# A fourth seven-product step of w_out in each late tile, the first product copied by ScalarE, and the casts placed one half step later

## The chip, the cores and the metric

The kernel runs on one core of one Trainium2 chip. The metric is the device time of one execution in microseconds (us), lower is better. Engines are named as the profile names them: PE is TensorE (matrix products, into PSUM), PEld its weight loads, DVE is VectorE, ACT is ScalarE, POOL is GpSimd, SP issues transfers.

## What is computed

The input has 8 batches of 3008 tokens of 256 numbers. A spectral mixing step (Fourier transform along the tokens, a complex 256x256 product with a bias, soft shrinkage, inverse transform) makes 24064 tokens, on which a dense two-layer network runs:

```python
def _moe_ref(x, w_in, w_out):          # x: 24064 x 256, w_in: 256 x 2048, w_out: 2048 x 256
    h = x @ w_in
    r = np.maximum(h, 0.0)
    g = r * r
    return (g @ w_out).astype(np.float32)

attn_out = _attn_ref(**attn_kwargs)    # rfft, complex product and bias, shrinkage, irfft
out = _moe_ref(x=attn_out.reshape(B * S, D), **moe_kwargs)
```

## The kernel before, in words

**Tiles and steps.** The tokens are cut into 48 tiles (six per batch) of 500 or 504 tokens, in two halves of `h` = 250 or 252. The 2048 hidden columns go in 8 steps of 256, so a tile has steps 0 to 7 and the program 384. Numbers are fp32; every product is made of three matrix products of reduced-precision parts ("high" and "low" parts of both sides, hence tiles in pairs such as `mg0`, `mg1`).

**One step.** The first product of a step is w_in times the tile. A 2x2 block product is made with seven block products instead of eight, by sums of blocks: `Step.first` issues four of them (12 matmuls into the PSUM banks psh0 and psh1), `Step.second` the other three (9 matmuls, psh2 and psh3). VectorE puts them together: it copies the first product to SBUF (`p1`, tile `mp`), adds it to the second (`u2`, tile `mu`), adds that to a pair (`v`, tile `mv`), and makes four rectified sums into the tile `mc`, by `rectified` (shown as CUSTOM_DVE_ANT_0 in the trace, as ISA in an instruction order). One of the four is made in `first`; in `second` there are two, first `c[:, 1:3]` from `psh2` and `v`, then `c[:, 0]` from `psh3` and `p1`. So `p1` is still read at the very end of `second`. The tile `mp` has one buffer (the table `MAIN` says `"mp": 1`). The end of `second` then gives out the casts: ScalarE squares `mc` in place and casts it to the high part `mg0`, GpSimd subtracts to get the low part `mg1`.

**w_out, plain and seven.** `Step.out` multiplies with w_out: 12 matmuls of 500 columns into the two accumulators `pso0` and `pso1`. It runs two half steps behind: in the main loop (one pass `m` per half step) TensorE gets `first` of step n, half of `out` of n - 2, the other half, `second` of n, and so on. In the tiles 38 to 46 (`FREE`), where the work of the mixing step is over, the steps in `SEVEN` (1, 3, 5) take seven block products here too (`out_seven`): 21 matmuls of 250 columns. They need four sums of the blocks of `mc`, which `forms` makes: three VectorE operations into `ftt`, two ScalarE casts to the high parts `fth`, two GpSimd subtractions to the low parts `ftl`. Parts of the seven products pile up over the tile in two banks (`psf`), and `tile_sums` (four VectorE operations into `mo`) unfolds them once, in the tile after; the last `out` of a tile then adds its accumulators (two VectorE operations on `mo`) and stores.

**Weights of the sums.** `out_sums(n)` makes, for each step in `SEVEN`, the sums of the w_out blocks: six GpSimd operations and one ScalarE cast, in the tiles before 38, placed by a time in a list of jobs.

**Next tile.** In the late tiles the input of the following tile is split into parts by `Tokens.free`, given out around the casts of steps 0, 2, 4 and 6, as pieces: sums `ts` at step 0, and at the later steps a ScalarE cast to `yt0` with a GpSimd subtraction to `yt1`.

**What sets the order.** `then` chains each operation behind the one given out before it on its engine, so within an engine the order is that of the program text; nothing on an engine overtakes.

Of the kernel before, what the change touches and what calls it, by code (L numbers as in the profile page):

```python
# [11 lines left out]
F32R = mybir.dt.float32r  # L12
# [20 lines left out]
NF = FF // 128  # L33
# [25 lines left out]
TURN0, TURNS, PACE = 92, J, 6  # L59
FREE = range(ENDS * len(HALF) + 2, B * len(HALF) - 1)  # L60
SPARE = 6
SEVEN = (1, 3, 5)


@with_exitstack
def fnet_moe(ctx: ExitStack, tc, x, w_r, w_i, b2, w_in, w_out, bm, cm, dx, am2, a32, c32, d32, out):
# [34 lines left out]
    def T(name, shape, dt, tag=None):  # L101
        tag = tag or name
        return pools.get(tag, phase["pool"]).tile(shape, dt, name=name, tag=tag, bufs=phase["bufs"].get(tag, 2))
# [72 lines left out]
    def halves(hi, lo, v, eng):  # L176
        copy(act, hi, v)
        sub(eng, lo, v, hi)
# [416 lines left out]
    class Tokens:  # L595
# [3 lines left out]
        def free(self, n, behind):  # L599
            y, h = raw[self.t], self.h  # L600
            if n == 0 and not behind:
                self.s = T("ts", [128, 1024], F32)[:, :4 * h].rearrange("p (j h) -> p j h", j=4)
                yts[self.t] = [
                    T(f"yt{j}", [128, 7 * HM], F32R)[:, :7 * h].rearrange("p (j h) -> p j h", j=7) for j in range(2)
                ]
            s = self.s
            if n == 0:
                if not behind:
                    then(pool, sub, pool, s[:, 0], y[:, 0, h:2 * h], y[:, 0, :h])
                    then(pool, sub, pool, s[:, 1], y[:, 1, h:2 * h], y[:, 0, h:2 * h])  # L610
                else:
                    then(pool, pool.tensor_add, out=s[:, 2], in0=y[:, 0, :h], in1=s[:, 1])
                    then(pool, sub, pool, s[:, 3], y[:, 1, :h], s[:, 2])
                return
            pieces = {
                (2, False): (B11, 1, y[:, 0, :h].unsqueeze(1)),
                (2, True): (B21, 2, y[:, 1, :2 * h].rearrange("p (j h) -> p j h", j=2)),
                (4, False): (T1, 2, s[:, 0:2]),
                (6, False): (T2, 2, s[:, 2:4]),
            }  # L620
            if (n, behind) in pieces:
                b, j, v = pieces[n, behind]
                js = slice(b, b + j)
                yh, yl = yts[self.t]
                then(act, copy, act, yh[:, js], v)
                then(pool, sub, pool, yl[:, js], v, yh[:, js])
# [53 lines left out]
    ws = []  # L680

    def out_sums(n):
        if not ws:
            ws.extend(T(name, [128, len(SEVEN), 4, 128], F32R) for name in ("wsh", "wsl"))
        i = SEVEN.index(n)
        st = T("st", [128, 1024], F32, tag="tt")
        w = st[:, :512].rearrange("p (f e d) -> p f e d", f=2, e=2)
        s = st[:, 512:].rearrange("p (j d) -> p j d", j=4)
        pool.tensor_add(out=st[:, :512].rearrange("p (f d) -> p f d", f=2), in0=wout[0][:, 2 * n:2 * n + 2], in1=wout[1][:, 2 * n:2 * n + 2])
        a11, a21, a12, a22 = w[:, 0, 0], w[:, 0, 1], w[:, 1, 0], w[:, 1, 1]  # L690
        pool.tensor_add(out=s[:, 0], in0=a21, in1=a22)
        sub(pool, s[:, 1], s[:, 0], a11)
        sub(pool, s[:, 2], a11, a21)
        sub(pool, s[:, 3], a12, s[:, 1])
        halves(ws[0][:, i], ws[1][:, i], s, pool)

    def tile_sums(t):
        h = tiles[t][2]
# [10 lines left out]
    class Step:  # L709
# [12 lines left out]
        def first(self):  # L722
            h = self.h
            self.ps = pa, pb, pc, pd = [bank([128, 2, 256], f"psh{j}")[:, :, :h] for j in range(4)]
            self.p1 = p1 = T("mp", [128, HM], F32)[:, :h]
            u2 = T("mu", [128, HM], F32)[:, :h]
            self.v = v = T("mv", [128, 2 * HM], F32)[:, :2 * h].rearrange("p (j h) -> p j h", j=2)
            self.c = c = T("mc", [128, 4 * HM], F32)[:, :4 * h].rearrange("p (j h) -> p j h", j=4)
            self.product(pa[:, 0], A11, B11)
            if self.t + self.n == 0:  # L730
                m4, m6, m3 = (pd[:, 0], A12, B21), (pc[:, 0], S4, B22), (pb[:, 0], S1, T1)
                m5, m2, m7 = (pb[:, 1], S3, T3), (pa[:, 1], S2, T2), (pc[:, 1], A22, T4)
                for m, terms in (
                    (m4, (0, 1, 2)), (m6, (0, 1, 2)), (m3, (0, 1)), (None, 4), (m2, (0, 1)), (m3, (2,)),
                    (m5, (0, 1, 2)), (m7, (0, 1)), (m2, (2,)), (m7, (2,)), (None, 3),
                ):
                    if m:
                        self.product(*m, terms)
                    else:
                        awake(terms, then)  # L740
            else:
                self.product(pa[:, 1], S2, T2)
                self.product(pb[:, 0], S1, T1)
                self.product(pb[:, 1], S3, T3)
            then(dve, copy, dve, p1, pa[:, 0])
            then(dve, dve.tensor_add, out=u2, in0=pa[:, 1], in1=p1)
            then(dve, dve.tensor_add, out=v, in0=pb, in1=u2.unsqueeze(1).broadcast_to([128, 2, h]))
            self.rectified(c[:, 3], pb[:, 0], v[:, 1])
# [4 lines left out]
        def second(self):  # L753
            h, c = self.h, self.c
            pc, pd = self.ps[2:]
            if self.end:
                return self.finish(pc, pd)
            if self.t + self.n:
                self.product(pc[:, 0], S4, B22)
                self.product(pc[:, 1], A22, T4)  # L760
                self.product(pd[:, 0], A12, B21)
            self.rectified(c[:, 1:3], pc, self.v)
            self.rectified(c[:, 0], pd[:, 0], self.p1)
            self.cut = last_of[dve]
            self.g = g = [
                T(f"mg{j}", [128, 4 * HM], F32R)[:, :4 * h].rearrange("p (j h) -> p j h", j=4) for j in range(2)
            ]
            then(act, act.activation, c, c, AF.Square)
            then(act, copy, act, g[0], c)
            self.bent = last_of[act]  # L770
            for j in (slice(0, 1), slice(2, 4)) if self.seven else (slice(0, 2), slice(2, 4)):
                then(pool, sub, pool, g[1][:, j], c[:, j], g[0][:, j])
            self.low = last_of[pool]
# [14 lines left out]
        def out_seven(self, j):  # L788
            t, h, n = self.t, self.h, self.n
            i, begins = SEVEN.index(n), n == self.sevens[0]  # L790
            if begins and j == 0:
                part[t] = [bank([128, 512])[:, :2 * h].rearrange("p (j h) -> p j h", j=2) for _ in range(2)]
            low, high = [a[:, :2 * h].rearrange("p (j h) -> p j h", j=2) for a in acc[t]]
            p16, p57 = part[t]
            f = 2 * n
            plain = [[w[:, f + k, d * 128:(d + 1) * 128] for w in wout] for d, k in ((0, 0), (0, 1), (1, 1))]
            sums = [[w[:, i, k] for w in ws] for k in range(4)]
            g, tf = self.g, (self.th, self.tl)
            if j == 0:
                todo = ((p16[:, 0], plain[0], g, 0), (low[:, 0], plain[1], g, 2), (low[:, 1], sums[3], g, 3))  # L800
            else:
                todo = (
                    (p57[:, 0], sums[0], tf, 0), (p57[:, 1], sums[2], tf, 1),
                    (p16[:, 1], sums[1], tf, 2), (high[:, 0], plain[2], tf, 3),
                )
            for q, (x, y) in enumerate(((0, 0), (1, 0), (0, 1))):
                for at, (ps, a, b, k) in enumerate(todo):
                    then(
                        pe, pe.matmul, ps, a[x], b[y][:, k],
                        start=begins and q == at == 0, stop=i == len(SEVEN) - 1 and q == 2 and j == 1 and at in (1, 2),  # L810
                    )
# [206 lines left out]
    for r in range(-1, len(units) + 3):  # L1018
# [5 lines left out]
        k = r - 2  # L1024
# [103 lines left out]
    for m in range(2 * len(steps) + 4):  # L1128
# [1 line left out]
        if k and 0 <= n - 2 < len(steps):  # L1130
            steps[n - 2].out(1)
        if n < len(steps):
            t, i = divmod(n, NF // 2)
            ahead = k and t in FREE and i in (0, 2, 4, 6)
            if ahead:
                if i == 0:
                    tokens = Tokens(t + 1)
                tokens.free(i, False)
            (steps[n].second if k else steps[n].first)()
            if ahead:  # L1140
                tokens.free(i, True)
            if not k and n and steps[n - 1].seven:
                steps[n - 1].forms()
            if not k and n % (NF // 2) == 0 and steps[n].t - 1 in FREE:
                tile_sums(steps[n].t - 1)
        if not k and 0 <= n - 2 < len(steps):
            steps[n - 2].out(0)
        if m in LATER:
# [103 lines left out]
```

## Time and profile before

| | |
|---|---|
| three runs, us | 2565.12, 2564.72, 2565.14; median 2565.12 |
| the profiled execution, us | 2564.88, of which its span is 2563.1 |
| TensorE busy | 2553.7 us (100%), its granted clock full throughout (9 in every slice) |
| VectorE, ScalarE, GpSimd busy | 74%, 55%, 68% |
| chain that ended last | 97% TensorE, 1% VectorE, 1% transfers |

"Busy" of an engine is the time in which one of its instructions runs. Matmuls are pipelined: a row's duration is longer than the pitch at which they follow each other, so lengths on TensorE are read from start to start. The same holds, by less than 0.1 us, for operations that follow each other on the other engines. Times in the trace count from the start of the span.

### The profile page before, as it was taken

The numbers are of one execution on the slowest core, as the hardware profiler recorded it, in microseconds if no ns is written. First come the engines' busy times: TensorE is split into PE (matmuls) and PEld (weight loads), VectorE is DVE, ScalarE is ACT, GpSimd is POOL, SyncE is SP. The second block draws the span as 40 slices with busy tenths as digits, with TensorE's granted clock in tenths as the row PEclk, the third lists the DMA queues.
The fourth block names the chain that finished last, engine by engine and source line by source line (L and its number), as shares of the span: only waits on it lengthen the run. The fifth ranks groups of instructions, "written<-read, shape, count | busy, mean of one in ns | idle before, by whom it ended". The sixth has DMA issues, their size and how long they took to land.

```text
span 2563.1 us, 47855 instructions
## 1 busy us (share of the span) xinstructions
PE 2553.7 (100%) x17453; PEld 2363.8 (92%) x17453; DVE 1889.7 (74%) x3767; ACT 1412.9 (55%) x2167; POOL 1746.1 (68%) x1672
## 2 busy tenths in 40 slices
PE   9999999999999999999999999999999999999999
PEld 7899999999999999999999999999999999999998
DVE  7876776777777777777677777777777566888886
ACT  5655555555555555555555555555555555555554
POOL 1167666676766777667676777776565857888885
PEclk9999999999999999999999999999999999999999
DMA  9633332333333333333333333333333451000000
GB/s 315 195 94 90 115 93 85 99 107 106 108 105 117 106 103 100 116 116 112 91 104 117 103 121 103 103 113 95 109 101 95 126 156 48 25 26 25 25 25 17
DMA packets 191121, 257.03 MB, mean 100 GB/s; under 512 B 18136, under 2 KB 137936, under 8 KB 190888
## 3 DMA queue, kind: packets, MB, share of 16 engines
q1 hardware_dynamic: 177473, 228.70, 28.8%
q0 software_dynamic: 13280, 25.16, 4.1%
q8 instruction: 140, 2.29, 0.4%
q14 instruction: 93, 0.76, 0.1%
q10 hardware_dynamic: 135, 0.12, 0.0%
HBM read 150.36 MB, written 103.55 MB: 99 GB/s over the span
## 4 chain that ended last, share of the span: by engine, by line
PE 97%; DVE 1%; DMA 1%; POOL 0%; ACT 0%; issue 0%; SPq 0%; DVEq 0%; ACTq 0%
PE pso L593 39%; PE psh L593 36%; PE psf L311 7%; PE psf L290 3%; PE psf L344 2%; PE psf L252 2%; PE psf L593 1%; PE psf L476 1%; PE psf L557 1%; PE psf L558 1%; PE psf L554 1%; PE psf L374 1%; PE psf L531 1%; PE psf L411 0%; PE psf L486 0%; PE psf L462 0%
## 5 line engine op out<-in xcount | busy, mean ns | idle before, releaser
L114 POOL TENSOR_TENSOR mg<-mc,mg 128x500 fp32r<-128x500 f32 (+1 forms) x766 | 995.2, 1320 | 427.9 <-ACT mg L110 344.2
L593 PE MATMUL pso<-mg,wout 128*128 128x500 f32 (+1 forms) x4365 | 1099.1, 389 | 0.8 <-POOL mg L114 0.8
L593 PE MATMUL psh<-yt,win 128*128 128x250 f32 (+1 forms) x8064 | 1074.2, 280 | 0.8 <-DVE mc L593 0.3
L593 PEld LDWEIGHTS psh<-yt,win 128*128 128x128 f32 x8064 | 1018.8, 189 | 27.7 <-DVE yt L114 0.6
L593 PEld LDWEIGHTS pso<-mg,wout 128*128 128x128 f32 x4365 | 781.0, 188 | 124.9 <-POOL mg L114 1.0
L593 ACT ACTIVATE mc<-mc 128x1000 f32<-128x1000 f32 (+1 forms) x384 | 400.5, 1043 | 447.3 <-DVE mc L593 446.2
L593 DVE CUSTOM_DVE_ANT_0 mc<-psh,mv 128x250 f32<-128x250 f32 (+3 forms) x769 | 418.6, 546 | 281.0 <-PE psh L593 239.1
L110 ACT CAST mg<-mc 128x1000 fp32r<-128x1000 f32 (+1 forms) x385 | 396.8, 1031 | 13.8
L593 DVE TENSOR_TENSOR mv<-psh,mu 128x500 f32<-128x500 f32 (+1 forms) x384 | 260.9, 679 | 47.0 <-PE psh L593 12.3
L311 PE MATMUL psf<-wx,kxh 128*128 128x256 f32 x1008 | 210.8, 281 | 0.0
L111 DVE COPY mp<-psh 128x250 f32<-128x250 f32 (+1 forms) x384 | 160.3, 417 | 54.3 <-PE psh L593 31.6
L332 DVE TENSOR_TENSOR kv<-psf,ke 64x256 f32<-64x256 f32 x336 | 141.7, 422 | 55.4 <-PE psf L311 41.5
L311 PEld LDWEIGHTS psf<-wx,kxh 128*128 128x128 f32 x1008 | 167.5, 189 | 2.7 <-DVE ke L323 0.2
L593 DVE TENSOR_TENSOR mu<-psh,mp 128x250 f32<-128x250 f32 (+1 forms) x384 | 160.9, 419 | 12.3
L110 ACT COPY dy<-psf 128x188 f32<-128x188 f32 (+2 forms) x229 | 71.4, 315 | 173.8 <-PE psf L558 173.3
L593 DVE CUSTOM_DVE_ANT_0 mc<-psh,mp 128x250 f32<-128x250 f32 (+1 forms) x384 | 156.9, 409 | 6.4 <-PE psh L593 6.2
L223 POOL TENSOR_TENSOR xs<-xt 120x256 f32<-120x256 f32 x156 | 120.4, 793 | 60.5 <-DMA xt<-x_in 23.3
L114 POOL TENSOR_TENSOR ksl<-kv,ksh 128x512 fp32r<-128x512 f32 x84 | 109.7, 1306 | 66.8 <-ACT ksh L110 60.0
L311 PE MATMUL psf<-wx,kxl 128*128 128x256 f32 x504 | 141.5, 281 | 0.0
L114 POOL TENSOR_TENSOR yt<-yr,yt 128x250 fp32r<-128x250 f32 (+1 forms) x94 | 88.4, 942 | 43.6 <-ACT yt L110 43.2
L334 ACT ACTIVATE kc<-kv,low 128x512 f32<-128x512 f32 x84 | 60.8, 724 | 88.4 <-DVE kv L332 88.3
L114 DVE TENSOR_TENSOR xl<-xs,xh 120x512 fp32r<-120x512 f32 x78 | 93.2, 1195 | 7.8 <-ACT xh L110 7.8
(164 smaller groups left out, 3055.7 us busy)
## 6 DMA issues: line engine op xcount, KB each, us to landing
ka<-s SPq DMA_DIRECT2D x96, 256.0 KB, 3.1
du<-s SPq DMA_DIRECT2D x86, 256.0 KB, 2.9
kcm<-cm_in POOLq DMA_DIRECT2D x84, 256.0 KB, 3.7
s<-kuh SPq DMA_DIRECT2D x84, 256.0 KB, 3.4
s<-kul SPq DMA_DIRECT2D x84, 256.0 KB, 3.6
s<-xe SPq DMA_DIRECT2D x82, 240.0 KB, 2.4
xt<-x_in SPq DMA_DIRECT2D x81, 240.0 KB, 3.2
out<-mo SPq DMA_DIRECT2D x64, 250.0 KB, 2.3
```

What stands on the lines that cost most here:

```text
L110: return act.copy(out=out, in_=in_)
L111: return eng.tensor_copy(out=out, in_=in_)
L114: return eng.tensor_tensor(out=out, in0=a, in1=b, op=ALU.subtract)
L223: return eng.tensor_tensor(out=out[:, :n], in0=self.xt[:, :n, 0], in1=self.xt[:, :n, 1], op=(ALU.add, ALU.subtract)[t])
L252: nc.tensor.matmul(ps[:, t], am_sb[0][:, j, t], v[:, t], start=n == 0, stop=n == 2)
L290: nc.tensor.matmul(pv[:, :, c, g, :], self.a[:, g, c * 128:(c + 1) * 128], bg, start=True, stop=True)
L311: self.last = nc.tensor.matmul(ps, l, wx[j][:, k, c, :], start=n == 0, stop=n == 5)
L332: dve.tensor_add(out=v[64 * r:64 * r + 64, g], in0=ps[gs], in1=self.e[gs, r])
L334: act.activation(r, v, AF.Relu, bias=low)
L344: nc.tensor.matmul(ps[:, g], self.cm[:, g, j * 128:(j + 1) * 128], r[:, g], start=n == 0, stop=n == 2)
L374: self.mm = nc.tensor.matmul(ps[:M1, t], nam if t and i else am32[:, t], self.xt[:, 0, i], start=i == 0, stop=i == 1)
L593: last_of[eng] = op(*args, **kwargs)
```

## The change

`SEVEN` gets a fourth member, step 6, so four of eight steps of the tiles 38 to 46 take the seven products for w_out. The sums of the weights of that step go into storage of the mixing weights (`wx`), which are read no more by then. In the tiles 38 to 47, ScalarE and not VectorE copies the first product to `mp`. The casts of a step leave `second` for a method of their own, which the main loop calls after `first` of the next step; with them move the pieces of the next tile (the last one from step 6 to behind the casts of step 4), and `tile_sums`, which now stands behind `first` of the new tile's step 1 and not of its step 0.

```diff
--- before.py
+++ after.py
@@ -59,7 +59,7 @@
 TURN0, TURNS, PACE = 92, J, 6
 FREE = range(ENDS * len(HALF) + 2, B * len(HALF) - 1)
 SPARE = 6
-SEVEN = (1, 3, 5)
+SEVEN = (1, 3, 5, 6)
 
 
 @with_exitstack
@@ -616,7 +616,7 @@
                 (2, False): (B11, 1, y[:, 0, :h].unsqueeze(1)),
                 (2, True): (B21, 2, y[:, 1, :2 * h].rearrange("p (j h) -> p j h", j=2)),
                 (4, False): (T1, 2, s[:, 0:2]),
-                (6, False): (T2, 2, s[:, 2:4]),
+                (4, True): (T2, 2, s[:, 2:4]),
             }
             if (n, behind) in pieces:
                 b, j, v = pieces[n, behind]
@@ -681,7 +681,9 @@
 
     def out_sums(n):
         if not ws:
-            ws.extend(T(name, [128, len(SEVEN), 4, 128], F32R) for name in ("wsh", "wsl"))
+            for j, name in enumerate(("wsh", "wsl")):
+                w = T(name, [128, 3, 4, 128], F32R)
+                ws.append([w[:, k] for k in range(3)] + [wx[j][:, 0].rearrange("p c (k d) -> p (c k) d", d=128)])
         i = SEVEN.index(n)
         st = T("st", [128, 1024], F32, tag="tt")
         w = st[:, :512].rearrange("p (f e d) -> p f e d", f=2, e=2)
@@ -692,7 +694,7 @@
         sub(pool, s[:, 1], s[:, 0], a11)
         sub(pool, s[:, 2], a11, a21)
         sub(pool, s[:, 3], a12, s[:, 1])
-        halves(ws[0][:, i], ws[1][:, i], s, pool)
+        halves(ws[0][i], ws[1][i], s, pool)
 
     def tile_sums(t):
         h = tiles[t][2]
@@ -742,7 +744,8 @@
                 self.product(pa[:, 1], S2, T2)
                 self.product(pb[:, 0], S1, T1)
                 self.product(pb[:, 1], S3, T3)
-            then(dve, copy, dve, p1, pa[:, 0])
+            eng = act if self.t >= FREE[0] else dve
+            then(eng, copy, eng, p1, pa[:, 0])
             then(dve, dve.tensor_add, out=u2, in0=pa[:, 1], in1=p1)
             then(dve, dve.tensor_add, out=v, in0=pb, in1=u2.unsqueeze(1).broadcast_to([128, 2, h]))
             self.rectified(c[:, 3], pb[:, 0], v[:, 1])
@@ -762,6 +765,11 @@
             self.rectified(c[:, 1:3], pc, self.v)
             self.rectified(c[:, 0], pd[:, 0], self.p1)
             self.cut = last_of[dve]
+            if self.t < FREE[0]:
+                self.casts()
+
+        def casts(self):
+            h, c = self.h, self.c
             self.g = g = [
                 T(f"mg{j}", [128, 4 * HM], F32R)[:, :4 * h].rearrange("p (j h) -> p j h", j=4) for j in range(2)
             ]
@@ -794,7 +802,7 @@
             p16, p57 = part[t]
             f = 2 * n
             plain = [[w[:, f + k, d * 128:(d + 1) * 128] for w in wout] for d, k in ((0, 0), (0, 1), (1, 1))]
-            sums = [[w[:, i, k] for w in ws] for k in range(4)]
+            sums = [[w[i][:, k] for w in ws] for k in range(4)]
             g, tf = self.g, (self.th, self.tl)
             if j == 0:
                 todo = ((p16[:, 0], plain[0], g, 0), (low[:, 0], plain[1], g, 2), (low[:, 1], sums[3], g, 3))
@@ -1130,19 +1138,21 @@
         if k and 0 <= n - 2 < len(steps):
             steps[n - 2].out(1)
         if n < len(steps):
-            t, i = divmod(n, NF // 2)
-            ahead = k and t in FREE and i in (0, 2, 4, 6)
-            if ahead:
-                if i == 0:
-                    tokens = Tokens(t + 1)
-                tokens.free(i, False)
             (steps[n].second if k else steps[n].first)()
-            if ahead:
-                tokens.free(i, True)
-            if not k and n and steps[n - 1].seven:
-                steps[n - 1].forms()
-            if not k and n % (NF // 2) == 0 and steps[n].t - 1 in FREE:
-                tile_sums(steps[n].t - 1)
+            t, i = divmod(n - 1, NF // 2)
+            if not k and t >= FREE[0]:
+                ahead = t in FREE and i in (0, 2, 4)
+                if ahead:
+                    if i == 0:
+                        tokens = Tokens(t + 1)
+                    tokens.free(i, False)
+                steps[n - 1].casts()
+                if ahead:
+                    tokens.free(i, True)
+                if steps[n - 1].seven:
+                    steps[n - 1].forms()
+                if i == 0 and t - 1 in FREE:
+                    tile_sums(t - 1)
         if not k and 0 <= n - 2 < len(steps):
             steps[n - 2].out(0)
         if m in LATER:
```

Three places show what that does to the engines' orders. The first is ScalarE over steps 5, 6 and 7 of a late tile; ACTIVATE is the square, `mg` and `fth` are the casts. Before:

```order
L593 ACTIVATE mc<-mc 128x1000
L110 CAST mg_28457<-mc 128x1000
L110 CAST fth<-ftt 128x500 x2
L110 CAST yt_28123<-ts 128x500
L593 ACTIVATE mc<-mc 128x1000
L110 CAST mg_28522<-mc 128x1000
L593 ACTIVATE mc<-mc 128x1000
L110 CAST mg_28584<-mc 128x1000
```

and now, steps 5, 6 and the start of 7:

```order
L110 COPY mp<-psh_28486 128x250
L593 ACTIVATE mc<-mc 128x1000
L110 CAST mg_28510<-mc 128x1000
L110 CAST fth<-ftt 128x500 x2
L110 COPY mp<-psh_28549 128x250
L593 ACTIVATE mc<-mc 128x1000
L110 CAST mg_28573<-mc 128x1000
L110 CAST fth<-ftt 128x500 x2
L110 COPY mp<-psh_28621 128x250
L593 ACTIVATE mc<-mc 128x1000
L110 CAST mg_28645<-mc 128x1000
```

A copy to `mp` stands ahead of each square: it is the first product of the step after the one that is squared. Step 6 has its `fth` casts, and the last `yt` cast is gone from here.

The second is GpSimd in the same steps. Before, from the `ftl` of step 3 to the `mg` of step 7:

```order
L114 TENSOR_TENSOR ftl<-ftt,fth 128x500 x2
L114 TENSOR_TENSOR yt_28124<-ts,yt_28123 128x500
L114 TENSOR_TENSOR mg_28396<-mc,mg_28395 128x500 x2
L114 TENSOR_TENSOR mg_28458<-mc,mg_28457 128x250
L114 TENSOR_TENSOR mg_28458<-mc,mg_28457 128x500
L114 TENSOR_TENSOR ftl<-ftt,fth 128x500 x2
L114 TENSOR_TENSOR yt_28124<-ts,yt_28123 128x500
L114 TENSOR_TENSOR mg_28523<-mc,mg_28522 128x500 x2
L114 TENSOR_TENSOR mg_28585<-mc,mg_28584 128x500 x2
```

and now:

```order
L114 TENSOR_TENSOR ftl<-ftt,fth 128x500 x2
L114 TENSOR_TENSOR yt_28180<-ts,yt_28179 128x500
L114 TENSOR_TENSOR mg_28447<-mc,mg_28446 128x500 x2
L114 TENSOR_TENSOR yt_28180<-ts,yt_28179 128x500
L114 TENSOR_TENSOR mg_28511<-mc,mg_28510 128x250
L114 TENSOR_TENSOR mg_28511<-mc,mg_28510 128x500
L114 TENSOR_TENSOR ftl<-ftt,fth 128x500 x2
L114 TENSOR_TENSOR mg_28574<-mc,mg_28573 128x250
L114 TENSOR_TENSOR mg_28574<-mc,mg_28573 128x500
L114 TENSOR_TENSOR ftl<-ftt,fth 128x500 x2
L114 TENSOR_TENSOR mg_28646<-mc,mg_28645 128x500 x2
```

Steps 5 and 6 now stand back to back as seven-product steps, and the last `yt` piece stands between the `mg` of step 4 and that of step 5.

The third is VectorE where a tile begins. The rows `mo<-psf` are the end of `tile_sums`, `mo<-pso` the two sums of the last `out`; `mc<-psh,mv 128x500` and `mc<-psh,mp` end a step. Before:

```order
L593 TENSOR_TENSOR mo<-psf,mu 128x500
L593 TENSOR_TENSOR mo<-psf,mo 128x250
L593 ISA mc<-psh_29104,mv 128x500
L593 ISA mc<-psh_29105,mp 128x250
L111 COPY mp<-psh_29170 128x250
L593 TENSOR_TENSOR mu<-psh_29170,mp 128x250
L593 TENSOR_TENSOR mv<-psh_29171,mu 128x500
L593 ISA mc<-psh_29171,mv 128x250
L593 TENSOR_TENSOR mo<-pso_28749,mo 128x500
L593 TENSOR_TENSOR mo<-pso_28750,mo 128x500
L593 ISA mc<-psh_29172,mv 128x500
L593 ISA mc<-psh_29173,mp 128x250
```

and now:

```order
L593 TENSOR_TENSOR mu<-psh_29216,mp 128x250
L593 TENSOR_TENSOR mv<-psh_29217,mu 128x500
L593 ISA mc<-psh_29217,mv 128x250
L111 COPY mo<-psf 128x250
L593 TENSOR_TENSOR mu<-psf,mo 128x250
L593 TENSOR_TENSOR mo<-psf,mu 128x500
L593 TENSOR_TENSOR mo<-psf,mo 128x250
L593 TENSOR_TENSOR mo<-pso_28795,mo 128x500
L593 TENSOR_TENSOR mo<-pso_28796,mo 128x500
L593 ISA mc<-psh_29218,mv 128x500
L593 ISA mc<-psh_29219,mp 128x250
```

The copies to `mp` are gone, and the four operations of `tile_sums` stand directly ahead of the two on `pso`, in one half step, all ahead of the end of step 1.

## Rows read from the trace of the kernel before

**Rows 1.** TensorE, timeline, tile 40: start us, us, engine, line, operation, tiles, count

```profile
2259.11 2.88 PE L593 MATMUL pso<-mg,wout 128*128 128x500 f32 x12
2261.82 2.60 PE L593 MATMUL psh<-yt,win 128*128 128x250 f32 x21
2264.26 0.28 PE L593 MATMUL psf<-mg,wout 128*128 128x250 f32 x1
...
2266.72 2.62 PE L593 MATMUL psh<-yt,win 128*128 128x250 f32 x21
```

**Rows 2.** VectorE in the timeline of tile 40, step 5

```profile
2257.57 0.68 DVE L593 CUSTOM_DVE_ANT_0 mc<-psh,mv 128x500 f32<-128x500 f32 x1 [0.61 <-PE psh L593]
2258.16 0.41 DVE L593 CUSTOM_DVE_ANT_0 mc<-psh,mp 128x250 f32<-128x250 f32 x1
2258.67 0.42 DVE L111 COPY mp<-psh 128x250 f32<-128x250 f32 x1
2259.12 0.42 DVE L593 TENSOR_TENSOR mu<-psh,mp 128x250 f32<-128x250 f32 x1
...
2260.83 0.67 DVE L114 TENSOR_TENSOR ftt<-mc 128x500 f32<-128x500 f32 x1
...
2263.67 0.67 DVE L593 CUSTOM_DVE_ANT_0 mc<-psh,mv 128x500 f32<-128x500 f32 x1
```

**Rows 3.** GpSimd in the timeline of the same step

```profile
2260.83 2.65 POOL L114 TENSOR_TENSOR mg<-mc,mg 128x250 fp32r<-128x250 f32 x2 [1.27 <-ACT mg L110]
2263.44 2.68 POOL L114 TENSOR_TENSOR ftl<-ftt,fth 128x500 fp32r<-128x500 f32 x2
```

**Rows 4.** Timelines of VectorE, GpSimd and TensorE, step 5 of tile 38

```profile
2179.35 1.13 DVE L114 TENSOR_TENSOR ftt<-mc 128x500 f32<-128x500 f32 x1
...
2179.23 2.38 POOL L114 TENSOR_TENSOR mg<-mc,mg 128x250 fp32r<-128x250 f32 x2 [1.27 <-ACT mg L110]
...
2184.00 1.27 POOL L114 TENSOR_TENSOR ftl<-ftt,fth 128x500 fp32r<-128x500 f32 x1 [0.99 <-ACT fth L110]
...
2182.66 0.28 PE L593 MATMUL psf<-mg,wout 128*128 128x250 f32 x1
...
2185.66 0.51 PE L593 MATMUL psh<-yt,win 128*128 128x250 f32 x3
```

**Rows 5.** ScalarE in the timeline of tile 40, step 5

```profile
2258.60 1.04 ACT L593 ACTIVATE mc<-mc 128x1000 f32<-128x1000 f32 x1 [1.68 <-DVE mc L593]
```

**Rows 6.** ScalarE's copies to `mo`, by tile name: shortest/median/longest ns, starts, shapes

```profile
L110 ACT COPY mo<-pso x78: 368/580/589, 174.7 to 2559.1; 128x500 f32<-128x500 f32 x49, 128x504 f32<-128x504 f32 x28, 128x250 f32<-128x250 f32 x1
```

**Rows 7.** Timelines of VectorE, GpSimd and TensorE where tile 41 begins

```profile
2270.88 0.41 DVE L111 COPY mo<-psf 128x250 f32<-128x250 f32 x1
...
2272.83 0.67 DVE L593 CUSTOM_DVE_ANT_0 mc<-psh,mv 128x500 f32<-128x500 f32 x1
...
2277.05 1.27 DVE L593 TENSOR_TENSOR mo<-pso,mo 128x500 f32<-128x500 f32 x2 [0.89 <-PE pso L593]
2278.23 0.67 DVE L593 CUSTOM_DVE_ANT_0 mc<-psh,mv 128x500 f32<-128x500 f32 x1
...
2284.11 2.68 POOL L114 TENSOR_TENSOR ftl<-ftt,fth 128x500 fp32r<-128x500 f32 x2
...
2284.71 0.28 PE L593 MATMUL psf<-mg,wout 128*128 128x250 f32 x1
```

**Rows 8.** GpSimd in the timeline of tile 40, steps 2 and 3

```profile
2247.05 2.52 POOL L114 TENSOR_TENSOR mg<-mc,mg 128x500 fp32r<-128x500 f32 x2
2249.52 1.08 POOL L114 TENSOR_TENSOR yt<-yr,yt 128x500 fp32r<-128x500 f32 x1
2250.79 2.66 POOL L114 TENSOR_TENSOR mg<-mc,mg 128x250 fp32r<-128x250 f32 x2 [0.19 <-ACT mg L110]
```

**Rows 9.** GpSimd's operations on `st` by tile name; its timeline afterwards

```profile
L689 POOL TENSOR_TENSOR st<-wout,wout x3: 1282/1286/1295, 2007.8 to 2036.4; 128x512 f32<-128x512 f32 x3
...
2060.29 2.51 POOL L114 TENSOR_TENSOR mg<-mc,mg 128x504 fp32r<-128x504 f32 x2 [3.38 <-ACT mg L110]
```

## The prediction

> **What bounds the kernel now.** Read TensorE's timeline in a late tile first: its rows follow each other without idle time [rows 1], so in the tiles 38 to 46 the end is set by how many columns are multiplied, unless some engine is late with an operand. A plain w_out step takes 2261.82 - 2259.11 = 2.71 us, a seven-product one 2266.72 - 2264.26 = 2.46, and the 21 products of w_in between them 2264.26 - 2261.82 = 2.44. Write S for the start of such a run of 21 (nine of `second` of a step, twelve of `first` of the next). S of step 5 is 2259.11 - 2.44 = 2256.67; the next S comes 2.44 + 2.71 = 5.15 later behind a plain `out`, 2.44 + 2.46 = 4.90 behind a seven.
>
> Second, how late the other engines may be. In a seven step VectorE's three `forms` operations start at 2260.83, S + 4.16 [rows 2]; GpSimd's four subtractions start at the same instant and end at 2263.44 + 2.68 = 2266.12, which is 5.29 after `forms` begin [rows 3]. In step 5 of tile 38 the last subtraction ended at 2184.00 + 1.27 = 2185.27 and the seven took 2185.66 - 2182.66 = 3.00, so TensorE lost 0.54 [rows 4]. The deadline is then 2185.27 - 0.54 = 2184.73, 2.07 after the seven begin. In the clean step it is 2264.26 + 2.07 = 2266.33, S + 9.66; GpSimd makes it by 0.21. At step 1 of tile 41 it ends at 2284.11 + 2.68 = 2286.79, with a deadline of 2284.71 + 2.07 = 2286.78: no margin at all [rows 7].
>
> Third, what `forms` wait for. VectorE has no idle time from 2258.16 to 2263.67, but for the handover ahead of `forms`; when they end, the end of the next step starts 2.84 after they began, at S + 1.85 and not the S + 0.90 of a step behind a plain one [rows 2].
>
> **The change, part by part.** *Fewer columns*: nine tiles, one step each, 9 x (2.71 - 2.46) = 2.25 us less [rows 1].
>
> *The copy on ScalarE.* VectorE's copy and its handover took 2259.12 - (2258.16 + 0.41) = 0.55, and that is not simply saved. `mp` has one buffer, and the last rectified sum of a step still reads it; the copy of the next step therefore waits for the end of that sum on VectorE, as it did when both stood on VectorE. No row shows this copy on ScalarE. The nearest is its shortest copy from PSUM, 0.37 for the same 250 columns [rows 6], and ScalarE starts 0.03 after VectorE's last sum today (2258.60 against 2258.57) [rows 2, 5]. With 0.03 + 0.37 + some 0.08 for the way back it is 0.48: a gain of 0.07, with bounds of 0.15 and -0.1. `forms` then start at S + 4.09. The square behind the copy starts some 0.3 to 0.4 later, and with it GpSimd's subtractions: `forms` get ahead of them by about that. In the clean step both start together and GpSimd's first pair takes 2.65 [rows 3]; in tile 38 GpSimd came 0.12 ahead, its pair took 2.38, and the first of `forms` took 1.13 instead of 0.67 [rows 2, 4]. So they take turns, and GpSimd would have waited for the first of `forms` in any case: I cost its later start at nothing. The two disturbed sevens of tile 38's kind (rows 4 are one; the timeline has one other, in tile 44) vanish: -2 x 0.54 = -1.1.
>
> The Trainium skill says why ("SBUF — State Buffer", "Who interferes with whom"): a VectorE operation with two SBUF inputs and a GpSimd one that reads SBUF exclude each other, and the second waits for the whole of the first; the 1.13 agrees. By that rule the waits on `yt` pieces below are real and the sum is the first of the two given there; were the port merely shared, it would be the second.
>
> *Step 6 behind step 5.* No seven step stands behind a seven today. The end of step 6 starts at 4.09 + 2.84 - 5.15 = S + 1.78; its `forms` come 2260.83 - 2257.57 - 0.07 = 3.19 later [rows 2], S + 4.97; GpSimd ends 5.29 behind that, S + 10.26. The deadline is 9.66 - 0.25 = S + 9.41, as the `out` ahead is itself a seven. TensorE waits 0.85. This is the cover that is gone: a plain step between sevens took up VectorE's lag.
>
> *`tile_sums` in step 1.* Today its four operations take 2272.83 - 2270.88 = 1.95 in step 0, where the slack is, and in step 1 VectorE idles 0.89 ahead of the two sums on `pso` [rows 7]. Now all six stand in step 1: ready at 2277.05 - 0.89 - 0.09 (operations overlap by this) - 0.07 = 2276.00, plus 1.95 plus the two sums' 2278.23 - 2277.05 = 1.18 gives 2279.13 and not 2278.23 for the end of the step: 0.90 later, 0.83 for `forms` after the copy's gain. Without margin that is TensorE's wait, 0.84, in the tiles 39 to 46.
>
> *What this passes on.* Behind that step 1 `forms` start at S + 5.24, so the end of step 2 starts at 5.24 + 2.84 - 5.15 = S + 2.93. The two sums take 1.0, the copy 0.4, ScalarE's `yt` cast ahead of the square another 0.4; the subtractions come 2260.83 - 2258.60 = 2.23 after the square's start [rows 3, 5], S + 6.95, last 2.5, and a `yt` piece of 1.08 follows [rows 8], done at S + 10.5. Step 3's S is 2.44 + 2.46 + 0.84 = 5.74 on: the piece runs until S + 4.7, over the 4.09 at which `forms` want to start. Today the piece ends 0.19 ahead of them [rows 8]. They start at 4.7, GpSimd ends at 10.0, and TensorE waits 0.33. The same sum for step 4, which now has a `yt` piece on either side of its subtractions, puts the second piece's end at S + 4.95 of step 5: a wait of 0.58, and step 6 is later by the 0.86, less what the 0.58 gives: 1.13 instead of 0.85.
>
> *Weights of step 6*: one more job on `st`, seven operations of which none on GpSimd is longer than 1.30 [rows 9], where GpSimd idles over 3 us a step [rows 9]. Costed at nothing; were it in the way, one wait of a us or so.
>
> **The sum.** Against the execution's own 2564.88 (span 2563.1, 0.2 below the median of 2565.12): steps 1, 3, 5 and 6 cost 0.84 + 0.33 + 0.58 + 1.13 = 2.88 in eight tiles, 23.0, and 0.85 in tile 38, which has no `tile_sums` ahead; less 2.25 and 1.1: +20.5, **2585.4**, I say 2585. Without the waits on `yt` pieces it is 8 x 0.84 + 9 x 0.85 - 3.35 = +11.0, 2576. I take the first, since today's 0.19 is less than the 0.7 by which the piece moves.
>
> **The rivals.** *(B) No turns lost on `yt` pieces*: 2576. *(C) One long wait only*: if `tile_sums` finds room, 9 x 0.85 - 3.35 = +4.3; if step 6 does, 8 x 0.84 - 3.35 = +3.4: about 2569. *(D) The cover holds, faster by a trifle*: were ScalarE's copy done while VectorE still makes the last sums, the 0.55 would leave VectorE's chain, `forms` would start some 0.5 sooner, and in a row of sevens or behind `tile_sums` the lag would gather less than the margin: -2.25 - 1.1 = 2562 (with the two disturbed steps kept, 2563). It decides at the start of the copy: ahead of the end of `mc<-psh,mp`, or behind. The single buffer speaks against it; for it, that the first product is ready by then. *(E) The order of turns flips*: where `forms` come behind a GpSimd subtraction as in rows 4, a seven loses 0.54 more and hands a us to the next; twice a tile that is another 10 or more: 2596 and up.
>
> **How the numbers follow.** The forecast has 0.42, B 0.22, C 0.14, D 0.11, E 0.11. The range, 2566 to 2598, leaves out D, a little of C and part of E. A measurement of this kernel tells some 0.2% (5 us, so 2560 to 2570) from no change: slower 0.42 + 0.22 + 0.11 = 0.75, within 0.24 (C and D), faster 0.01, since the columns saved and every wait of today together do not come to 5 us.
>
> **What would show it.** In the timeline after: ScalarE's `mp` copy starts some 0.03 to 0.1 behind the end of `mc<-psh,mp`, and the square behind it; step 6's end at S + 1.8 or later; six `mo` operations in a row ahead of step 1's end; TensorE idle ahead of products on `ftl` at steps 1 and 6 above all, released by GpSimd; plain steps unchanged. I am wrong if the copies start ahead of that sum, if the sevens of steps 1 and 6 still take 2.46, or if GpSimd's four subtractions at step 6 end earlier than 5.2 after `forms` begin.

## The result and the profile after

The changed kernel takes 2582.44 us (median of six runs, 2582.08 to 2584.57) against 2565.13 before (2564.72 to 2565.68): 17.3 us slower, ratio 1.0069 with a 95% interval of 1.0056 to 1.0081. The forecast was 2585, so direction and size hold. The profiled execution is the slowest of the six, 2584.57 with a span of 2582.8. Its 2 us more lie ahead of tile 38: the first seven-product step starts at 2165.09 in it, at 2162.55 in the trace of before.

The page of the kernel after: busy time, the chain of work that ended last, and one row of the costliest groups.

```profile
PE 2561.4 (99%) x17534; PEld 2369.6 (92%) x17534; DVE 1890.2 (73%) x3714; ACT 1446.5 (56%) x2266; POOL 1765.0 (68%) x1696
...
PE 84%; POOL 6%; DVE 5%; ACT 2%; issue 2%; DMA 1%; ACTq 0%; DVEq 0%; POOLq 0%; SPq 0%
...
L311 PE MATMUL psf<-wx,kxh 128*128 128x256 f32 x1008 | 211.0, 281 | 2.2 <-DVE kp L301 2.2
```

The chain was 97% TensorE and 1% VectorE; now GpSimd holds 6% of it and VectorE 5%: TensorE waits for GpSimd, and GpSimd's work for VectorE's. The last row, of the mixing work, had no idle time before and has 2.2 us here: most of the profiled run's 2 us.

The waits of the kernel after from tile 38 to the end (waiting engine, tile and line, released by, us in total, times, longest):

```profile
ACT mp L110 <- DVE mc L593: 53.3, 52, 3.9
DVE mu L593 <- ACT mp L110: 41.5, 80, 2.5
...
PEld psf L593 <- POOL ftl L114: 14.7, 27, 0.7
PE psf L593 <- POOL ftl L114: 9.0, 19, 0.5
...
PEld psf L593 <- ACT fth L110: 2.6, 9, 0.4
```

Before, the third of these was 0.7 us in two times (the disturbed sevens of [rows 4]). The first two are the new copy: ScalarE waits for VectorE, then VectorE for ScalarE.

Tile 40 on TensorE, kernel after, to be laid beside [rows 1]. A run of 21 products on `psh` ends where the `out` behind it starts, and a seven-product step, a "seven" for short, lasts from its first `psf` product to the next run on `psh`:

```profile
2241.42 2.60 PE L593 MATMUL psh<-yt,win 128*128 128x250 f32 x21
...
2249.01 0.28 PE L593 MATMUL psf<-mg,wout 128*128 128x250 f32 x1
...
2252.26 2.60 PE L593 MATMUL psh<-yt,win 128*128 128x250 f32 x21
...
2259.85 0.28 PE L593 MATMUL psf<-mg,wout 128*128 128x250 f32 x1
...
2262.42 2.59 PE L593 MATMUL psh<-yt,win 128*128 128x250 f32 x21
2264.84 2.88 PE L593 MATMUL pso<-mg,wout 128*128 128x500 f32 x12
2267.56 2.60 PE L593 MATMUL psh<-yt,win 128*128 128x250 f32 x21
2270.00 0.28 PE L593 MATMUL psf<-mg,wout 128*128 128x250 f32 x1
...
2272.75 2.60 PE L593 MATMUL psh<-yt,win 128*128 128x250 f32 x21
2275.19 0.28 PE L593 MATMUL psf<-mg,wout 128*128 128x250 f32 x1
...
2278.74 2.61 PE L593 MATMUL psh<-yt,win 128*128 128x250 f32 x21
```

The sevens take 2252.26 - 2249.01 = 3.25, 2.57, 2.75 and 3.55 us at steps 1, 3, 5 and 6. Clean is 2.46, so they lose 0.80, 0.12, 0.30 and 1.09; the plain step still takes 2.72. **Lost time** below is this difference (start to start, less 2.455) summed over the tiles 38 to 46:

| kernel | step 1 | step 3 | step 5 | step 6 | sum |
|---|---|---|---|---|---|
| before | 0.29 | 0.50 | 0.49 | plain | 1.28 |
| after | 6.30 | 1.17 | 2.89 | 10.32 | 20.68 |

20.68 - 1.28 less 2.25 of columns saved is 17.15; the medians differ by 17.31. So the waits at the sevens make up the loss but for 0.16 us, and the weights of step 6, costed at nothing, cost nothing that shows.

### The profile page after: what moved, and what is told of

Same layout as the page of the kernel before. It is cut to its first block, busy times and chain, and to the rows that moved or that the text cites. A ratio compares the mean times of both kernels' runs of the same rounds, so it can differ in the third digit from the quotient of the medians.

```text
span 2582.8 us, 48095 instructions
## 1 busy us (share of the span) xinstructions
PE 2561.4 (99%) x17534; PEld 2369.6 (92%) x17534; DVE 1890.2 (73%) x3714; ACT 1446.5 (56%) x2266; POOL 1765.0 (68%) x1696
## 4 chain that ended last, share of the span: by engine, by line
PE 84%; POOL 6%; DVE 5%; ACT 2%; issue 2%; DMA 1%; ACTq 0%; DVEq 0%; POOLq 0%; SPq 0%
PE pso L593 33%; PE psh L593 30%; PE psf L311 7%; POOL mg L114 3%; PE psf L290 3%; POOL ftl L114 3%; PE psf L344 2%; PE psf L252 2%; DVE mc L593 1%; PE psf L476 1%; PE psf L557 1%; PE psf L558 1%; DVE ftt L114 1%; PE psf L554 1%; ACT mg L110 1%
## 5 line engine op out<-in xcount | busy, mean ns | idle before, releaser
L114 POOL TENSOR_TENSOR mg<-mc,mg 128x500 fp32r<-128x500 f32 (+3 forms) x766 | 988.3, 1310 | 429.8 <-ACT mg L110 341.6
L593 PE MATMUL pso<-mg,wout 128*128 128x500 f32 (+2 forms) x4284 | 1080.9, 388 | 0.6 <-POOL mg L114 0.6
L593 PEld LDWEIGHTS pso<-mg,wout 128*128 128x128 f32 x4284 | 767.1, 189 | 120.8 <-POOL mg L114 0.9
L593 DVE TENSOR_TENSOR mu<-psh,mp 128x250 f32<-128x250 f32 (+1 forms) x384 | 160.9, 419 | 51.1 <-ACT mp L110 41.5
L111 DVE COPY mp<-psh 128x250 f32<-128x250 f32 (+1 forms) x304 | 126.7, 417 | 45.8 <-PE psh L593 31.2
```

The lines of the kernel that those rows point to most:

```text
L111: return eng.tensor_copy(out=out, in_=in_)
L114: return eng.tensor_tensor(out=out, in0=a, in1=b, op=ALU.subtract)
L593: last_of[eng] = op(*args, **kwargs)
```

## The experiments

All kernels compute the whole result. Ratios are against the kernel before on the same chip, with 95% intervals. The last four columns are the lost time in us, from the one execution of each kernel that was profiled; -0.06 is nine clean steps, which are some 0.007 shorter than the 2.455 taken off.

| kernel | us | ratio | step 1 | step 3 | step 5 | step 6 |
|---|---|---|---|---|---|---|
| e1_three | 2574.85 | 1.0034 [1.0021, 1.0047] | 6.28 | 1.27 | 2.92 | plain |
| e4_sums_late | 2572.08 | 1.0025 [1.0015, 1.0034] | 7.78 | -0.06 | 0.50 | plain |
| e3_copy_dve | 2579.91 | 1.0053 [1.0038, 1.0068] | 7.91 | -0.06 | 0.50 | 9.38 |
| e2_mp2 | 2572.24 | 1.0023 [1.0014, 1.0033] | 2.67 | -0.06 | -0.06 | 3.68 |
| e10_late_mp | 2568.01 | 1.0011 [1.0002, 1.0020] | 2.66 | -0.06 | -0.06 | 3.91 |
| e5_pieces | 2575.43 | 1.0037 [1.0024, 1.0051] | 6.30 | -0.06 | -0.06 | 7.77 |
| e8_sums | 2577.51 | 1.0045 [1.0033, 1.0058] | 1.98 | 1.21 | 2.82 | 10.03 |
| e6_all | 2564.70 | 0.9997 [0.9988, 1.0005] | -0.06 | -0.06 | -0.06 | 3.26 |
| e7_all3 | 2564.04 | 0.9993 [0.9984, 1.0002] | -0.06 | -0.06 | -0.06 | plain |
| e9_behind | 2561.66 | 0.9986 [0.9977, 0.9996] | -0.06 | -0.06 | -0.06 | none |

**One part of the change undone or done alone.** Three sevens, all else as in the kernel after:

```diff
-SEVEN = (1, 3, 5, 6)
+SEVEN = (1, 3, 5)
```

> The changed kernel with the old three seven steps (1, 3, 5); ScalarE's copy, the later casts and tile_sums in step 1 stay. Theory (VectorE's lag meets GpSimd's deadline): the 10.3 us of waits at step 6 go, 2.25 us of columns come back, the waits at step 1 (6.3 us, 0.8 in each of eight tiles) and at steps 3 and 5 (4.1) stay: 2574 us, and step 1's seven still takes 3.2. Rival (GpSimd has simply too much work with four sevens): all waits shrink together, step 1's below 0.3, 2566 us.

2574.85, as expected: the fourth seven costs 7.6 us by the medians (10.3 lost for 2.25 saved makes 8.1), and the steps 1, 3 and 5 lose what they lost with it. `tile_sums` alone, in the kernel before:

```diff
-            if not k and n % (NF // 2) == 0 and steps[n].t - 1 in FREE:
+            if not k and n % (NF // 2) == 1 and steps[n].t - 1 in FREE:
```

> The kernel before with one move: tile_sums behind the first sums of a tile's step 1 and not of its step 0. Theory: the six mo operations then delay the end of step 1 by 0.9 us, forms with them, and TensorE waits about 0.9 in step 1 of eight tiles: 2572 us, step 1's seven at 3.3 and the other two at 2.46. Rival (VectorE's 0.89 of idle time there takes it in): 2565 us.

2572.08, as expected: eight steps lose 0.93 to 1.04 each. Steps 3 and 5 lose nothing here, where the copy is VectorE's and the casts stand where they were. The copy alone put back on VectorE:

```diff
-            eng = act if self.t >= FREE[0] else dve
-            then(eng, copy, eng, p1, pa[:, 0])
+            then(dve, copy, dve, p1, pa[:, 0])
```

> The changed kernel with the copy back on VectorE; four sevens, later casts and tile_sums in step 1 stay. Theory: the single buffer made both copies wait for the same sum, so the place hardly matters: VectorE's chain is some 0.06 longer in each step, 1 to 4 us more in all, 2583 to 2587. Rival 1 (ScalarE's copy relieves VectorE): 9 us slower or more, 2592. Rival 2 (ScalarE's copy is what costs, since it delays the square): 2570 or less.

A miss: 2579.91 is 2.5 us faster than the kernel after, not slower (2579.36 to 2580.49 against 2582.08 to 2584.57, and 17.74 us lost against 20.68). Step 1 gains from ScalarE's copy (6.30 against 7.91), but steps 3 and 5 are clean without it (the 0.50 is one disturbed seven in tile 38, as in [rows 4]), and step 6, which inherits nothing, loses 9.38 and not 10.32. VectorE's and GpSimd's rows of this run at step 3 of tile 40 (`ftt` is the first of `forms`):

```profile
2255.73 0.67 DVE L114 TENSOR_TENSOR ftt<-mc 128x500 f32<-128x500 f32 x1
```

```profile
2254.50 1.07 POOL L114 TENSOR_TENSOR yt<-yr,yt 128x500 fp32r<-128x500 f32 x1
2255.73 2.66 POOL L114 TENSOR_TENSOR mg<-mc,mg 128x250 fp32r<-128x250 f32 x2 [0.16 <-ACT mg L110]
```

The `yt` piece ends at 2255.57, 0.16 ahead of `forms`, as in [rows 8]; `forms` run in 0.67. With ScalarE's copy it does not (kernel after, VectorE, then GpSimd, steps 3 and 5):

```profile
2256.32 1.08 DVE L114 TENSOR_TENSOR ftt<-mc 128x500 f32<-128x500 f32 x1
...
2266.49 1.25 DVE L114 TENSOR_TENSOR ftt<-mc 128x500 f32<-128x500 f32 x1
```

```profile
2255.79 1.07 POOL L114 TENSOR_TENSOR yt<-yr,yt 128x500 fp32r<-128x500 f32 x1
...
2259.36 2.67 POOL L114 TENSOR_TENSOR ftl<-ftt,fth 128x500 fp32r<-128x500 f32 x2
...
2266.14 1.06 POOL L114 TENSOR_TENSOR yt<-ts,yt 128x500 fp32r<-128x500 f32 x1
```

`forms` start while the piece runs and take 1.08 and 1.25 where 0.67 would do. So the copy pushes ScalarE's square back, the square GpSimd's pieces, and the pieces VectorE's `forms`.

**The pieces.** Both parts of a step's `yt` ahead of its casts (the loop over the two tables is left out):

```diff
-                (2, True): (B21, 2, ...),
-                (4, True): (T2, 2, s[:, 2:4]),
+            more = {(2, False): (B21, 2, ...), (4, False): (T2, 2, s[:, 2:4])}
```

> The changed kernel with both parts of the next tile's input (yt) of a step given out ahead of that step's casts, at steps 2 and 4. Theory (a yt subtraction of GpSimd that is under way when forms want to start holds the first of them, because the two take turns): the lost time of the sevens falls at step 3 from 1.17 us to about 0, at step 5 from 2.89 to 0 to 0.5, at step 6, which inherits step 5's lag, from 10.3 to about 8, and stays at step 1 (6.3): 2576 to 2577.5. Rival (GpSimd simply has too much to do in these steps, wherever the pieces stand): no change, 2581 to 2584. Second rival: pieces ahead hold up the casts of the plain steps 2 and 4, whose products then wait: above 2584.

2575.43, some 0.6 below the theory's range: step 5 lost nothing at all, and step 6 7.8 where about 8 was expected. The same VectorE group by shape, the kernel after first, then this one (busy us, mean ns):

```profile
L114 DVE TENSOR_TENSOR ftt<-mc 128x500 f32<-128x500 f32 x28 | 25.6, 913 | 0.0
```

```profile
L114 DVE TENSOR_TENSOR ftt<-mc 128x500 f32<-128x500 f32 x28 | 18.8, 672 | 0.0
```

Same 28 operations, same operands, 913 against 672 ns: only the place of the pieces differs, on ScalarE and GpSimd. GpSimd does as many subtractions as before, so its throughput is not the limit.

**The buffer.** Two buffers for `mp`, in the whole program:

```diff
-    "ms": 1, "mp": 1, "mu": 1, ...
+    "ms": 1, "mp": 2, "mu": 1, ...
```

> The changed kernel with two buffers for the tile mp, so that ScalarE's copy need not wait for the last rectified sum of the step before. Theory: VectorE's wait of 0.49 for the copy goes, 0.39 of every step's chain, so forms start 0.4 earlier in a clean step and 0.8 earlier behind a lag: the waits at steps 1 and 6 fall below 0.4 and those at 3 and 5 to nearly nothing, 2563 to 2569 us. Rival (the lag is that of forms and tile_sums alone, the copy is beside it): the waits stay as they are, 2580 us or more.

2572.24, above the range, although the late tiles did what was expected (6.2 lost), but for two of the nine waits at step 6, 0.6 each. The first seven of tile 38 came at 2167.79 in this trace, at 2162.55 before: 5 us were lost ahead of it. The waits from 1960 to 2060 us show a row that the kernel before does not have there:

```profile
PEld psh L593 <- ACT yt L110: 1.5, 1, 1.5
```

The traces show why: ahead of 2150 us VectorE's order of instructions differs from that of the kernel after in 389 of 3134 places, ScalarE's in 220 of 1901 and GpSimd's in 118 of 1380. The operations that `then` chains keep their order, as the section on the kernel before says; the mixing work between them, which is not chained, moved when the buffer was added. To settle that this costs the time, a second buffer in the late tiles alone:

```diff
-    "ms": 1, "mp": 1, "mu": 1, ...
+    "ms": 1, "mp": 1, "mq": 1, "mu": 1, ...
-LATE = ("wsh", "wsl", "tt", "th", "tl", "ts")
+LATE = ("wsh", "wsl", "tt", "th", "tl", "ts", "mq")
-            self.p1 = p1 = T("mp", [128, HM], F32)[:, :h]
+            self.p1 = p1 = T("mq" if self.t >= FREE[0] and self.n % 2 else "mp", [128, HM], F32)[:, :h]
```

> The changed kernel with a second buffer for the first product in the tiles 38 to 47 alone (odd steps use a tile of their own, mq); ahead of tile 38 nothing changes. With two buffers throughout, the sevens lost 2.67 us at step 1, nothing at steps 3 and 5 and 3.68 at step 6, but 4 to 5 us were lost ahead of tile 38. Theory (the excess of that run came from the mixing work whose order the second buffer changed, not from the late tiles): 2582.44 - 20.68 + 6.2 = 2568, range 2567 to 2569. Rival (the second buffer costs something in the late tiles that the sevens do not show): 2572 again.

2568.01, as expected, and ahead of 2150 us no instruction of the three engines stands elsewhere than in the kernel after: this one buffer gives back 14.4 of the 17.3 us.

**The sums.** `tile_sums` behind `second` of step 0:

```diff
+            if k and n % (NF // 2) == 0 and steps[n].t - 1 in FREE:
+                tile_sums(steps[n].t - 1)
-                if i == 0 and t - 1 in FREE:
-                    tile_sums(t - 1)
```

> The changed kernel with tile_sums given out behind second of a tile's step 0 and not behind first of step 1; the last products of step 6 are issued before that point, so it is allowed there. Theory (VectorE stands idle in step 0 and again 0.89 ahead of the sums on pso, so the four operations are free there and cost 0.9 of lag in step 1): the lost time of step 1 falls from 6.3 us to 0 to 0.5, that of steps 3 and 5 by up to half, step 6 by a few tenths: 2574 to 2576. Rival (VectorE is behind after step 6 and step 7 anyway, so the same work just moves the lag on): step 1 still loses 0.4 or more per tile, 2579 or above.

2577.51, between theory and rival: step 1 falls from 6.30 to 1.98, not to zero, and steps 3 and 5 do not move at all; why is said below, under what this passes on.

**All three remedies**, with four sevens and with three:

> Four seven-product steps with all three remedies: the parts of the next tile ahead of the casts, tile_sums behind second of step 0, and a second buffer for mp in the late tiles alone (odd steps use a tile of their own), so that the order of the mixing work ahead of tile 38 stays. Theory (the loss has these causes and no other): steps 1, 3 and 5 lose nothing, step 6 about 0.41 in nine tiles, as with two buffers before (3.7), against 1.28 lost in the kernel before and 2.25 fewer: 2565.12 + 3.7 - 1.28 - 2.25 = 2565.3, range 2564 to 2567. Rival (seven products in four steps ask for more of VectorE and GpSimd than a tile has): 2569 or above.

> The same three remedies with sevens in steps 1, 3 and 5 alone. Theory: every seven takes 2.46, so the 1.28 us that the kernel before loses go: 2563.8, range 2563.2 to 2564.6. Rival (the casts given out half a step later cost something by themselves): 2566 or above.

2564.70 and 2564.04, both within the theory's range, and neither to be told from the kernel before. With three sevens nothing is lost, so the late casts cost nothing by themselves. With four, step 6 alone loses, 0.36 each, which is more than the fourth seven saves (3.26 against 2.25); the waits of that kernel from tile 38 on:

```profile
DVE mu L593 <- ACT mp L110: 9.3, 21, 0.5
...
PEld psf L593 <- POOL ftl L114: 2.7, 9, 0.4
```

VectorE's wait for the copy has fallen from 41.5 us to 9.3 (and 1.8 for `mq`); left on TensorE are nine waits, one a tile, for GpSimd's subtractions. The second half of these seven products can be issued later:

```diff
+        wait = k and 0 <= n - 2 < len(steps) and steps[n - 2].seven and steps[n - 2].n == 6
-        if k and 0 <= n - 2 < len(steps):
+        if k and 0 <= n - 2 < len(steps) and not wait:
             steps[n - 2].out(1)
         if n < len(steps):
             (steps[n].second if k else steps[n].first)()
+            if wait:
+                steps[n - 2].out(1)
```

> Four sevens with the three remedies, and the second half of step 6's seven products (those on fth and ftl) issued behind second of the next tile's step 0 and not ahead of it, which puts 1.05 us of other products ahead of them. Theory (what is left at step 6 is GpSimd's last subtraction coming 0.36 too late): step 6 loses nothing, 2564.7 - 3.3 = 2561.4, range 2560.8 to 2562.6. Rival (tile_sums, which now must wait for these products, put VectorE behind for the next tile's step 1): step 1 loses some 0.3 in eight tiles, 2563.5 to 2565.

2561.66, as expected. TensorE at step 6 of tile 40 in this run:

```profile
2268.86 0.28 PE L593 MATMUL pso<-mg,wx 128*128 128x250 f32 x1
2268.98 1.21 PE L593 MATMUL psh<-yt,win 128*128 128x250 f32 x9
2270.02 0.52 PE L593 MATMUL psf<-fth,wx 128*128 128x250 f32 x3
...
2270.96 0.52 PE L593 MATMUL psf<-ftl,wx 128*128 128x250 f32 x3
```

The first product on `ftl` follows 0.94 behind the first on `fth`, which is eight products of 0.117: no wait. This run's waits have no row of TensorE for `ftl` left, and 2565.13 - 2.25 - 1.28 = 2561.6 is the time that was measured, to the tenth. This version is faster than the kernel before, by a little, 0.14% (0.04 to 0.23), and 2.4 us faster than the same with three sevens (e7_all3): here the fourth seven gives what its columns are worth.

## Why the prediction was right, and where its sizes were off

The mechanism held: VectorE's lag, GpSimd's deadline, TensorE's wait. Term by term, the sum put 6.7 us at step 1, 2.6 at step 3, 4.6 at step 5 and 9.9 at step 6; the trace has 6.30, 1.17, 2.89 and 10.32. The 3 us between 2585.4 and 2582.44 come from the two middle terms. That the profiled execution stands still nearer, at 2584.57, is luck, since some 2 us of it were lost ahead of tile 38. The two disturbed sevens went, as forecast.

**Bound and deadline: right.** GpSimd's last subtraction must end within 2.07 us of a seven's start; this gives every wait of tile 40. Step 6, kernel after, VectorE and then GpSimd:

```profile
2269.92 0.67 DVE L593 CUSTOM_DVE_ANT_0 mc<-psh,mv 128x500 f32<-128x500 f32 x1
...
2273.07 0.67 DVE L114 TENSOR_TENSOR ftt<-mc 128x500 f32<-128x500 f32 x1
```

```profile
2275.69 2.65 POOL L114 TENSOR_TENSOR ftl<-ftt,fth 128x500 fp32r<-128x500 f32 x2
```

GpSimd ends at 2278.34, 5.27 behind `forms` (5.29 was used), the deadline is 2275.19 + 2.07 = 2277.26, and the difference of 1.08 is the 1.09 that TensorE lost.

**Step 6 behind step 5: right.** 1.13 predicted, 1.09 measured in tile 40, 10.32 in nine tiles (9.9 predicted). Where step 5 hands nothing on (e5_pieces) it is 0.86 a tile, against 0.85. Forms came at S + 5.51 (2273.07 - 2267.56) and not at S + 5.83, as step 5 handed on less, but step 5's wait was shorter by about as much, so the difference stayed. Tile 38 lost 1.12 where 0.85 was put, and tile 43 1.49, of which some 0.4 is an idle time of VectorE ahead of `mv` whose cause stays open. The chain of waits was VectorE, GpSimd, TensorE. One thing was not seen: `fth` is late too (the 2.6 us in nine times above), but GpSimd is later, so it adds nothing.

**`tile_sums`: right.** 0.84 predicted in each of eight tiles, 0.73 to 0.85 measured. VectorE, kernel after, step 1 of tile 40, against [rows 7]:

```profile
2240.32 0.41 DVE L111 COPY mo<-psf 128x250 f32<-128x250 f32 x1
...
2242.27 1.25 DVE L593 TENSOR_TENSOR mo<-pso,mo 128x500 f32<-128x500 f32 x2
2243.44 0.67 DVE L593 CUSTOM_DVE_ANT_0 mc<-psh,mv 128x500 f32<-128x500 f32 x1
2244.03 0.41 DVE L593 CUSTOM_DVE_ANT_0 mc<-psh,mp 128x250 f32<-128x250 f32 x1
2244.92 0.42 DVE L593 TENSOR_TENSOR mu<-psh,mp 128x250 f32<-128x250 f32 x1 [0.49 <-ACT mp L110]
...
2246.60 0.67 DVE L114 TENSOR_TENSOR ftt<-mc 128x500 f32<-128x500 f32 x1
```

Six operations on `mo` in a row, the 0.89 of idle time gone, and `forms` at 2246.60 - 2241.42 = S + 5.18 (5.24 predicted).

**The copy: right, its handovers by luck.** ScalarE, same place:

```profile
2244.52 0.37 ACT L110 COPY mp<-psh 128x250 f32<-128x250 f32 x1 [3.85 <-DVE mc L593]
2244.79 1.04 ACT L593 ACTIVATE mc<-mc 128x1000 f32<-128x1000 f32 x1
```

It starts 0.08 behind the end of `mc<-psh,mp` (2244.44), so the single buffer does hold it. `mu` follows that sum's start by 0.89, before by 0.96: the gain is the predicted 0.07. But 0.03 was put for the way to ScalarE and 0.08, which no row showed, for the way back; they measured 0.08 and 0.03 (2244.89 to 2244.92), and the two errors cancel. The square starts 0.35 behind the sum's end, not 0.03. That GpSimd's subtractions start later for it was put at nothing, and at steps 1 and 6 that holds: they end 5.26 and 5.27 behind the start of `forms`. For the pieces the copy stood in the sum, with 0.4, and there it is needed for the loss: without it steps 3 and 5 lose nothing (e3_copy_dve).

**Turns on the pieces: right in kind, about twice too large.** Steps 3 and 5 lost 1.17 and 2.89, where 0.33 and 0.58 in eight tiles make 2.6 and 4.6. The term that was off is the end of the piece. At step 3 it was put at S + 4.7 (the terms of that sum as they are printed make 4.8: 10.53 less 5.74) and was at 2256.86 - 2252.26 = S + 4.60; at step 5 at S + 4.95, and was at 2267.20 - 2262.42 = S + 4.78. Whole durations of ScalarE's copy and cast (0.4 and 0.4) stood in the sum, where the next operation starts 0.27 behind the copy's start and 0.30 behind the cast's. (Operations on ScalarE thus overlap by 0.10 to 0.11, a little more than the 0.1 that the section on time and profile allows.) Beyond that, the first of `forms` ended 0.54 behind the piece's recorded end in both steps (2257.40 and 2267.74), not 0.67: VectorE had 0.13 of it done by then, or GpSimd's recorded end is that rough, which the traces leave open. Together that is 0.2 at step 3 (0.33 to 0.12) and 0.3 at step 5 (0.58 to 0.30), counted from the printed 4.7 and 4.95.

**What this passes on: right, and it has a limit.** Tile 38 has no `tile_sums` ahead, so its step 1 lost nothing. TensorE, GpSimd and VectorE of the kernel after at its step 3:

```profile
2167.55 2.61 PE L593 MATMUL psh<-yt,win 128*128 128x250 f32 x21
```

```profile
2170.76 1.08 POOL L114 TENSOR_TENSOR yt<-yr,yt 128x500 fp32r<-128x500 f32 x1
```

```profile
2171.62 0.76 DVE L114 TENSOR_TENSOR ftt<-mc 128x500 f32<-128x500 f32 x1
```

The piece ends at 2171.84, S + 4.29, and `forms` lose 0.09, which the margin takes up. In tile 40, behind a late step 1, it ended at S + 4.60. At step 5 it is S + 4.59 in tile 38 and S + 4.78 in tile 40. Steps 3 and 5 lost 0.00 and 0.08 in tile 38, 0.07 to 0.30 and 0.28 to 0.55 in the other eight. The traces of e1_three and e8_sums show the same for their tile 38. So step 1's lag does make the pieces late, by 0.2 to 0.3 between tiles 38 and 40. More of it does not make them later: TensorE's wait moves the next S too, so only the part of the lag that TensorE does not wait for is handed on. In e8_sums step 1 still lost 0.15 or more in each of the eight tiles, had thus no margin left, and handed on the same; that is why steps 3 and 5 did not move there. The lag alone is not enough either: in e3_copy_dve step 1 lost 0.9 or more, but without ScalarE's copy the pieces were early enough.

**Rivals.** B (no turns) was wrong by steps 3 and 5, 4.1 us directly, and by what step 6 inherits: without them it loses 2.6 less (e5_pieces). C was wrong, both waits are there. D's condition, a copy ahead of the last sum's end, is met in e10_late_mp (at step 2 of tile 40 the copy starts at 2245.34 and the sum ends at 2245.70); it gave 2568 and not the 2562 of the rival, as steps 1 and 6 still lose 0.3 to 0.7. E did not occur: at steps 1 and 6 `forms` still start ahead of GpSimd's subtractions, at step 1 of tile 40 by 0.43 (2246.60 against 2247.03).

**The remedies don't add.** Alone they give 14.4 (buffer), 7.0 (pieces) and 4.9 (sums), 26.3 in all, which is more than the 20.7 lost; together they give 17.7. The table shows the overlap: the buffer and the pieces each clear steps 3 and 5 by themselves, the buffer and the sums each take over half of step 1's loss. A step loses only what is left of its lag above the margin.

## What to carry to other kernels

An operation moved to a free engine gains only what its operands and its buffer allow: where the destination has one buffer that the old engine still reads, the chain through it gets hardly shorter (0.07 of 0.55 us here), and what stands behind it on the new engine is delayed. Where a chain has 0 to 0.2 us to spare, write down for each step the deadline and the lag that the step ahead hands on, and put optional work where an engine stands idle; waits of 0.1 to 1.1 us a step made a saving of 2.25 us into a loss of 17, three moves gave that loss back, and a fourth, later products for the last late operand, gave the saving. A buffer added for one stage should be added in that stage alone.

## What the runs showed of the hardware

- VectorE's first operation of `forms`, two inputs in SBUF, took 0.67 us when no GpSimd operation was under way at its start, or one started with it, and in tile 40 1.08 and 1.25 behind a `yt` subtraction under way. The Trainium skill's rule ("SBUF — State Buffer", "Who interferes with whom"), that the later of two such operations waits for the whole of the earlier, agrees to within the 0.13 us above: the first of `forms` ended 0.54 behind the subtraction.
- ScalarE copies 128x250 from PSUM in 0.37 us where VectorE takes 0.42, with 0.08 and 0.03 of waiting ahead and behind (2244.44 to 2244.52, 2244.89 to 2244.92) against 0.10 and 0.03 on VectorE (2258.57 to 2258.67, 2259.09 to 2259.12 in [rows 2]). The detour gains 0.07.
- A second buffer for a tile of 1 KB a partition cost some 4 us in a stage in which it was not needed (2572.24 in e2_mp2 against 2568.01 in e10_late_mp), by the other order of the work there.
